# Five groups of the first attention pass get a second load of x in strips of 32 channels, turned on VectorE, and GpSimd folds softmax sums

## The chip, the cores and the metric

The kernel runs on one core of a Trainium2 chip as one program. Its time is the device time of one execution in microseconds (us). Engines: PE is TensorE (matmuls; PEld is its weight loads), DVE is VectorE, ACT is ScalarE, POOL is GpSimd, SP is SyncE, which issues nearly all DMAs. Each engine works through its own list of instructions in a fixed order.

## The reference, cut to what matters

The work is an induced-set attention over x (4 batches, 11456 tokens, 128 channels, float32) with 32 inducing rows, and behind it a mixture of experts (8 experts) for the tokens whose skip score is positive:

```python
def mab(q, kv):
    s = scale * (q @ kv.transpose(0, 2, 1))
    s = s - s.max(-1, keepdims=True)
    a = np.exp(s)
    a /= a.sum(-1, keepdims=True) + 1e-09
    return a @ kv
h = mab(I, x)                 # 32 rows per batch: first pass over x
x = mab(x, h)                 # every token against h: second pass over x
do_compute = x @ w_skip > 0
e_idx = argmax(x[do_compute] @ w_gate); gate_w = its softmax probability
out = x; out[do_compute] += gate_w * (relu(x @ w1[e]) @ w2[e])
```

The host lays x out transposed, xT[b, channel, token], and the output is written transposed too.

## The kernel before, in words

A batch has 11456 tokens, cut into 5 groups of 2048 and one of 1216 (NG = 6). The tile of a group holds 128 channels on the partitions and its tokens in the free dimension; four streams of 512 tokens (Q = 4) are worked on together, so that 4 times 32 inducing rows fill 128 partitions. The names of the steps:

- `load` (line 353): two DMAs of 512 KB per group into a tile `x`. There are XB = 12 such tiles, the groups of two batches. A tile is free again when the second pass has read it.
- `first`: scores `I x` (PE, line 372), running maxima per partition (DVE, 378), exponentials `a` (ACT, 382). For the sum `a x`, tokens must lie on the partitions. So `xt` turns x with 16 PE transposes of 128x128 (407) into PSUM banks, and four copies bring them into an SBUF tile `xt` (`xtc`: ACT line 335 or DVE line 337). `aT` turns `a` with four PE transposes (391), and one copy brings it into `a1T`. `hsum` (417) multiplies the two, and `add` (426) accumulates with a rescaling by `f`.
- `middle`, once a batch: brings the four streams' maxima together, makes `h` (`hr`, and `hc` turned), chooses the batch's expert (DVE, line 536, called the choose here), lets SP load that expert's weights `w1s`, `w2s` by the number just found, and makes the expert's rows `yr`.
- `second`, for each group: scores (PE, 693), a transpose in blocks of 32x32 (DVE, 698), row maxima (700), the subtraction (704, POOL or DVE), exponentials (ACT, 707), their sum and its reciprocal (DVE, 711, 713), the normalisation (716, POOL or DVE), a transpose back (721), then the gate of the expert (`..._q`) and the scaling by it (820).
- `emit`: eight matmuls a group (872) into four banks, four copies `o` to SBUF (335 or 337), two stores (882).

What sets the order: every step is an `Op` with a cost for each engine that may run it. `best_order` reads a rank and a bias for each step from the string PLACES (three characters a step), and `in_order` places the steps one by one, choosing the engine where two are offered and giving out banks and buffers. The result is one fixed list for each engine; nothing is chosen at run time. The list is written for the whole program at once, so the second pass of one batch runs beside the first pass of the next. SP's list holds loads, stores and the weights in one order, and SP waits at each for what it needs.

In the rows of an order below, `x4` means four such instructions, `x_1_818` is a tile of group 1 (the last number only tells tiles apart), and `a_2_1_...` belongs to batch 2, group 1.

Of the kernel before, what the change touches and what calls it, by code (L numbers as in the profile page):

```python
# [16 lines left out]
P = 128  # L17
# [122 lines left out]
def best_order(ops, bufs):  # L140
# [44 lines left out]
def kernel(  # L185
# [39 lines left out]
    def bank(i):  # L225
        return banks[i]
# [97 lines left out]
    def act(w):  # L324
        return {"ACT": 0.22 + 0.37 * w / 512}
# [15 lines left out]
    def load(k, after):  # L341
        b, g = divmod(k, NG)
        s = bt[b]
        G = s.groups[g]
        st = Steps(k)
        buf = s.xbuf[g] = Buf("x")
        cut = G.s1[1:] if k == 0 else [GC // 2]
        cut = [0] + [c for c in cut if c < G.cols] + [G.cols]

        def go(o):  # L350
            t = s.x[g] = xp.tile([P, GC], F32, tag="x", name=f"x_{b}_{g}")
            for c, d in zip(cut, cut[1:]):
                nc.sync.dma_start(out=t[:, c:d], in_=xT[b, :, G.col0 + c:G.col0 + d])

        s.xin[g] = last["x"] = st.add({"SP": 0.08 * len(cut)}, go, after, behind=[last["x"]], take=[buf], size=G.cols * 0.512)
        return st


    def first(s, g):
# [88 lines left out]
    def middle(s):  # L448
# [222 lines left out]
    def second(s, G, x, main):  # L671
# [474 lines left out]
```

## Time and profile before

| | before |
|---|---|
| median of 3 runs | 225.86 us (225.54 to 226.64) |
| the profiled execution | 226.54 us, of which its span is 224.7 us |
| PE busy | 201.1 us (89% of the span) |
| DVE busy | 170.5 us (76%) |
| ACT busy | 140.8 us (63%) |
| POOL busy | 111.0 us (49%) |
| moved by DMA | 51.64 MB, mean 230 GB/s |
| mean granted clock of TensorE | 0.981 |

The span is what the trace covers; 1.8 us of the profiled execution lie outside it. A busy share is an average over the span. The program has five parts here, cut at the four chooses (line 536, at 42.0, 84.2, 140.3 and 178.4 us): stage 0 up to the first choose, stages 1 to 3 between chooses, stage 4 from the last choose to the end. In stage 0 first passes run, in stages 1 to 3 the second pass of one batch beside the first of the next, in stage 4 second passes.

### The profile page before, as it was taken

The numbers are of one execution on the slowest core, as the hardware profiler recorded it, in microseconds if no ns is written. First come the engines' busy times: TensorE is split into PE (matmuls) and PEld (weight loads), VectorE is DVE, ScalarE is ACT, GpSimd is POOL, SyncE is SP. The second block draws the span as 40 slices with busy tenths as digits, with TensorE's granted clock in tenths as the row PEclk, the third lists the DMA queues.
The fourth block names the chain that finished last, engine by engine and source line by source line (L and its number), as shares of the span: only waits on it lengthen the run. The fifth ranks groups of instructions, "written<-read, shape, count | busy, mean of one in ns | idle before, by whom it ended". The sixth has DMA issues, their size and how long they took to land.

```text
span 224.7 us, 6693 instructions
## 1 busy us (share of the span) xinstructions
PE 201.1 (89%) x2541; PEld 116.2 (52%) x2542; DVE 170.5 (76%) x444; ACT 140.8 (63%) x333; POOL 111.0 (49%) x284
## 2 busy tenths in 40 slices
PE   4899999989999999999999999989999979688630
PEld 1556767657368764543675647327585333233210
DVE  4363653659898997799888787989898989997640
ACT  2356476655598886766996864768785756346730
POOL 7000000222538668457366541357677879989610
PEclk9999999999999999999999999999999999999975
DMA  6999970086796027979993492454221867445692
GB/s 160 378 419 405 412 313 13 6 266 203 248 392 239 3 115 249 297 308 355 370 414 150 190 314 98 141 234 190 93 101 42 330 205 285 190 175 198 252 365 71
DMA packets 16614, 51.64 MB, mean 230 GB/s; under 512 B 1984, under 2 KB 4928, under 8 KB 16576
## 3 DMA queue, kind: packets, MB, share of 16 engines
q1 hardware_dynamic: 16288, 51.12, 61.4%
q8 instruction: 22, 0.36, 0.7%
q14 instruction: 16, 0.13, 0.2%
q10 hardware_dynamic: 288, 0.02, 0.1%
HBM read 27.68 MB, written 23.46 MB: 228 GB/s over the span
## 4 chain that ended last, share of the span: by engine, by line
PE 54%; POOL 11%; DVE 11%; DMA 10%; ACT 5%; issue 4%; SPq 1%; DVEq 0%; ACTq 0%; POOLq 0%
PE bank L407 16%; PE bank L872 12%; PE bank L417 8%; PE bank L372 6%; DMA w1s<-in_w_dram 4%; PE bank L391 3%; DMA x<-in_xT_dram 3%; ACT o L335 3%; PE bank L693 3%; DMA out_dram<-o 3%; POOL e L716 2%; POOL v L820 2%; DVE ts L700 2%; DVE e L698 2%; PE bank L778 2%
## 5 line engine op out<-in xcount | busy, mean ns | idle before, releaser
L407 PE MATMUL bank<-ident,x 128*128 128x128 f32 (+1 forms) x368 | 50.8, 281 | 1.0 <-DMA x<-in_xT_dram 0.8
L335 ACT COPY o<-bank 128x512 f32<-128x512 f32 (+1 forms) x80 | 40.9, 570 | 16.4 <-PE bank L872 14.4
L335 ACT COPY xt<-bank 128x512 f32<-128x512 f32 (+1 forms) x78 | 42.9, 591 | 10.9 <-PE bank L407 10.6
L704 POOL TENSOR_TENSOR e<-e,ts 128x512 f32<-128x512 f32 (+1 forms) x22 | 22.5, 1023 | 49.6 <-DVE cmx L536 37.5
L407 PEld LDWEIGHTS bank<-ident,x 128*128 128x128 f32 (+1 forms) x368 | 40.4, 141 | 12.7 <-issue 3.0
L872 PE MATMUL bank<-u,hr 32*128 32x512 f32 (+1 forms) x192 | 26.0, 608 | 3.4 <-ACT o L335 2.5
L716 POOL TENSOR_TENSOR e<-texp,ts 128x512 f32<-128x512 f32 (+1 forms) x19 | 18.9, 999 | 17.0 <-DVE ts L713 13.0
L820 POOL TENSOR_TENSOR v<-e,gs 128x512 f32<-128x512 f32 (+1 forms) x20 | 20.8, 1040 | 8.9 <-DVE gs L337 4.9
L417 PE MATMUL bank<-xt,a1T 128*32 128x129 f32 (+1 forms) x736 | 25.1, 275 | 0.0
L382 ACT ACTIVATE a<-bank,bias 128x512 f32<-128x512 f32 (+1 forms) x24 | 16.0, 666 | 14.5 <-DVE a L378 14.5
L372 PE MATMUL bank<-x,iT_sb 128*32 128x512 f32 (+1 forms) x192 | 24.8, 583 | 0.0
L872 PE MATMUL bank<-u,yr 32*128 32x512 f32 (+1 forms) x192 | 23.9, 565 | 0.7 <-DVE u L721 0.6
L417 PEld LDWEIGHTS bank<-xt,a1T 128*32 128x32 f32 (+1 forms) x736 | 19.3, 109 | 8.1 <-issue 3.8
L693 PE MATMUL bank<-x,hc 128*32 128x512 f32 (+1 forms) x192 | 22.8, 573 | 0.1
L707 ACT ACTIVATE texp<-e 128x512 f32<-128x512 f32 (+1 forms) x24 | 14.6, 609 | 10.9 <-POOL e L704 8.0
L378 DVE TENSOR_SCALAR_CACHE_REDUCE a<-bank,bias 128x512 f32<-128x512 f32 (+1 forms) x20 | 13.9, 693 | 5.5 <-PE bank L372 5.2
L698 DVE STREAM_TRANSPOSE e<-bank 128x512 f32<-128x512 f32 (+1 forms) x24 | 15.9, 664 | 2.1 <-PE bank L693 2.0
L721 DVE STREAM_TRANSPOSE u<-v 128x512 f32<-128x512 f32 (+1 forms) x24 | 15.9, 664 | 1.7 <-POOL v L820 1.6
L721 DVE STREAM_TRANSPOSE u<-e 128x512 f32<-128x512 f32 (+1 forms) x24 | 15.6, 661 | 1.1 <-POOL e L716 0.9
L700 DVE TENSOR_REDUCE ts<-e 128x16 f32<-128x512 f32 (+1 forms) x24 | 15.7, 653 | 0.8
L711 DVE TENSOR_REDUCE sums<-texp 128x16 f32<-128x528 f32 (+1 forms) x24 | 15.6, 648 | 0.9 <-ACT texp L707 0.9
L872 PEld LDWEIGHTS bank<-u,yr 32*128 32x128 f32 x192 | 9.8, 185 | 10.8 <-issue 5.8
(153 smaller groups left out, 293.9 us busy)
## 6 DMA issues: line engine op xcount, KB each, us to landing
x<-in_xT_dram SPq DMA_DIRECT2D x43, 512.0 KB, 8.1
out_dram<-o SPq DMA_DIRECT2D x40, 512.0 KB, 3.9
out_dram<-o SPq DMA_DIRECT2D x8, 304.0 KB, 4.7
w1s<-in_w_dram SPq DMA_DIRECT2D x4, 512.0 KB, 4.2
w2s<-in_w_dram SPq DMA_DIRECT2D x4, 512.0 KB, 4.9
x<-in_xT_dram SPq DMA_DIRECT2D x4, 152.0 KB, 2.8
x<-in_xT_dram SPq DMA_DIRECT2D x3, 96.0 KB, 9.1
iT_sb<-in_iT_dram ACTq DMA_DIRECT2D x1, 16.0 KB, 2.2
```

Of the source, the lines that this page charges most:

```text
L335: nc.scalar.copy(out=out, in_=in_)
L372: nc.tensor.matmul(ps[q * M:(q + 1) * M, 0:W], lhsT=iT_sb, rhs=s.x[g][:, G.s1[q]:G.s1[q] + W], start=True, stop=True)
L407: nc.tensor.transpose(out=px[0:w, q * P:(q + 1) * P], in_=s.x[g][:, o:o + w], identity=ident)
L417: nc.tensor.matmul(ph[q * M:(q + 1) * M, 0:P + 1], lhsT=st["aT"][0:w, i, q * M:(q + 1) * M], rhs=xts[bx.idx][0:w, i, q, :], start=(i == 0) ...
L693: nc.tensor.matmul(ps[q * M:(q + 1) * M, 0:W], lhsT=s.hc[:, 0:M], rhs=x()[:, G.s2[q]:G.s2[q] + W], start=True, stop=True)
L698: nc.vector.transpose(out=t[:, 0:W], in_=st["ps"][:, 0:W])
L700: nc.vector.tensor_reduce(out=mx[:, 0:nb], in_=blocks(t), axis=AX.X, op=ALU.max)
L704: on(o).tensor_tensor(out=blocks(t), in0=blocks(t), in1=wide(st["mx"]), op=ALU.subtract)
L716: on(o).tensor_tensor(out=blocks(st["e"]), in0=ev(M), in1=wide(st["i"]), op=ALU.mult)
L721: nc.vector.transpose(out=st[f"u{k}"][:, 0:W], in_=st[src][:, 0:W])
L820: on(o).tensor_tensor(out=blocks(u), in0=blocks(st["e"]), in1=wide(st["gm"]), op=ALU.mult)
L872: nc.tensor.matmul(bank(bp[q].idx)[:, 0:G.w1], lhsT=m[r, :], rhs=st[k][r, c], start=(k == "u1"), stop=(k == "u2"))
```

## The change

Batch 1's group 2 and groups 1 and 3 of batches 2 and 3 (STRIPS) are loaded a second time, into a tile `xq`: four DMAs, each into 32 partitions, which hold channel r, r + 32, r + 64 and r + 96 of one stream side by side. With that layout, transposes in blocks of 32x32 on DVE write the very tile `xt` that the PE transposes and copies made (`x_turned`, two instructions of 1024 elements a partition). `a` is turned by DVE as well (`a_turned`). As a 32x32 transpose keeps the streams apart and puts tokens in another order, all four streams of such a group use one maximum: `turn_bias` (PE), `least` (DVE), `spread` (PE) and `common` (ACT or DVE) make it, ahead of the exponentials. The number of x tiles goes from 12 to 10. `fold` may add the right half of a row's exponentials to the left half on POOL, so that DVE's sum reads 17 numbers per row in place of 33. PLACES is a new string for the whole program.

```diff
-    XB = min(12, 2 * NG)
+    XB = min(10, 2 * NG)
+    STRIPS = ((), (2,), (1, 3), (1, 3))
+            G.strips = G.g in STRIPS[b]
 PLACES = (
-    "6f04O07A08w08i07W4EO0Au2CN0BE07Z09L0CF0Dj0GS0Fj04V0BK09N0881AW0BU0EL06z4Fr0FV37b0As0BP02a06H00304q02F06Q05F23V01Q18B0603"
+    "Ez0Ad0DG09c0B70EU4FS0Bx3BB0HB4BM0Aq2CR09B0B50As02R08l07F07U3B209e3BJ07714n07t03b0AM12k05T02502n02A02w01H03z00u00w11U01F1"
...
+        if G.strips:
+            def strips(o):
+                t = G.xq_t = wk.tile([P, Q, GC // Q], F32, tag="xq", bufs=BUFS["xq"], name=f"xq_{b}_{g}")
+                for q in range(Q):
+                    c = G.col0 + G.s1[q]
+                    nc.sync.dma_start(out=t[q * M:(q + 1) * M], in_=xT[b, :, c:c + G.w1].rearrange("(i r) n -> r i n", i=Q))
+            G.xq_in = last["xq"] = st.add({"SP": 0.08 * Q}, strips, behind=[s.xin[g], last["xq"]], take=[G.xq], size=G.cols * 0.95)
...
+        def a_turned(o):
+            nc.vector.transpose(out=t.rearrange("p t c -> p (t c)"), in_=st["a"][:, 0:W])
+        def x_turned(o, h):
+            n = GC // Q // M // 2
+            nc.vector.transpose(out=xts[bx.idx][:, 2 * h:2 * h + 2, :, 0:P].rearrange("p i q (c r) -> p (i q) c r", c=Q),
+                                in_=G.xq_t.rearrange("p c (j n) -> p j c n", n=M)[:, n * h:n * (h + 1)])
...
+        if G.strips:
+            o = L.add({"PE": 0.2}, turn_bias, o_m, take=[f1])
+            o = L.add({"DVE": 0.27}, least, o, free=[f1])
+            o = L.add({"PE": 0.3}, spread, o, take=[f2])
+            o_m = o_b = L.add({"ACT": 0.2, "DVE": 0.17}, common, o, free=[f2])
...
+        def fold(o):
+            st["whole"] = o.eng == "DVE"
+            if not st["whole"]:
+                v = ev(2 * HALF)
+                nc.gpsimd.tensor_tensor(out=blocks(st["e"])[:, :, 0:HALF], in0=v[:, :, 0:HALF], in1=v[:, :, HALF:], op=ALU.add)
```

The order around batch 2's group 1 on PE before: two of its four transposes of x (line 407, `x_1_818`; the others stand further up), the turning of its `a` (391), and its sum (417).

```order
L503 MATMUL bank_72<-ident,hr_1230 128x128
L407 MATMUL bank_75<-ident,x_1_818 128x128 x4
L811 MATMUL bank_73<-lt_3_1173,rep 32x16 x4
L407 MATMUL bank_77<-ident,x_1_818 128x128 x4
L811 MATMUL bank_74<-lt_2_1012,rep 32x16 x4
L906 MATMUL bank_72<-ident,lo_1244 1x128
L391 MATMUL bank_73<-ident,a_2_1_1129 128x128 x4
L522 MATMUL bank_75<-ws_sb,hc_1266 128x8
L523 MATMUL bank_75<-ws_sb,hc_1266 128x9
L913 MATMUL bank_72<-lom_1285,ones 128x1
L372 MATMUL bank_77<-x_2_882,iT_sb 32x512 x4
L417 MATMUL bank_72<-xt_165,a1T_1_1277 32x129 x16
```

The same group on PE now, from the batch's middle (540) on: 403 is `turn_bias`, 412 is `spread`, and no row of lines 447 or 431 (the transposes of x and a) belongs to group 1.

```order
L540 MATMUL bank_76<-acc_690,rep 128x129
L403 MATMUL bank_73<-ident,bias_1_1217 1x128
L431 MATMUL bank_72<-ident,a_2_0_1103 128x128 x4
L840 MATMUL bank_70<-u_0_5_1079,lrq_171 32x128 x4
L387 MATMUL bank_77<-x_2_913,iT_sb 32x512 x4
L557 MATMUL bank_71<-ident,hr_1257 128x128
L412 MATMUL bank_73<-ones,mn_2_1_1268 32x1 x4
L457 MATMUL bank_72<-xt_166,a1T_0_1241 32x129 x16
```

The sixteen transposes of x and four of a are gone from PE, and two short steps stand in their place, the second of them behind a DVE step. On DVE, ahead of batch 2's middle (`den_2108`), before:

```order
L337 COPY o_5_0_2066<-bank_77 128x304
L337 COPY o_5_1_2074<-bank_76 128x304
L426 SCALAR_TENSOR_TENSOR acc_1225<-acc_1225,f_2_5_1941,bank_72 128x129
L337 COPY o_5_1_2074<-bank_74 128x304
L936 TENSOR_REDUCE marks<-gxs 128x1
L337 COPY gs_2_163<-bank_75 128x16
L378 TENSOR_SCALAR a_3_3_2084,bias_3_2100<-bank_71,bias_2_2044 128x512
L490 TENSOR_SCALAR den_2108<-bank_75 128x1
```

On DVE, ahead of the same middle (`den_1974`) now; 424 is `x_turned`:

```order
L466 SCALAR_TENSOR_TENSOR acc_1326<-acc_1326,f_2_5_1832,bank_73 128x129
L783 STREAM_TRANSPOSE u_1_2_1947<-v_1_2_1927 128x512
L424 STREAM_TRANSPOSE xt_167<-xq_1_1631 128x8x128 x2
L544 TENSOR_SCALAR den_1974<-bank_75 128x1
L545 RECIPROCAL den_1974<-den_1974 128x1
L864 TENSOR_REDUCE gs_1_159<-qexp_124 128x16
```

Three copies `o` left DVE here, and both halves of batch 3's group 1 are turned directly in front of the middle. On SP, the loads of batch 3 and the weights of batch 2 before (`x_3_1834` is group 3; 882 are stores):

```order
L353 DMA x_3_1834<-in_xT_dram 128x1024 x2
L353 DMA x_4_1849<-in_xT_dram 128x1024 x2
L882 DMA out_dram<-o_3_0_1893 128x1024
L882 DMA out_dram<-o_3_1_1910 128x1024
L882 DMA out_dram<-o_1_0_1985 128x1024
L353 DMA x_5_2026<-in_xT_dram 128x1024
L353 DMA x_5_2026<-in_xT_dram 128x192
L882 DMA out_dram<-o_1_1_2009 128x1024
L882 DMA out_dram<-o_5_0_2066 128x2x304
L882 DMA out_dram<-o_5_1_2074 128x2x304
L547 TENSOR_LOAD ei_2172
```

On SP now (368 is the second load, 945 are stores):

```order
L358 DMA x_1_1609<-in_xT_dram 128x1024 x2
L368 DMA xq_1_1631<-in_xT_dram 32x4x512 x4
L358 DMA x_2_1696<-in_xT_dram 128x1024 x2
L945 DMA out_dram<-o_0_0_1723 128x1024
L945 DMA out_dram<-o_0_1_1728 128x1024
L358 DMA x_3_1773<-in_xT_dram 128x1024 x2
L368 DMA xq_3_1782<-in_xT_dram 32x4x512 x4
L945 DMA out_dram<-o_1_0_1839 128x1024
L945 DMA out_dram<-o_1_1_1868 128x1024
L945 DMA out_dram<-o_3_1_1977 128x1024
L945 DMA out_dram<-o_3_0_1967 128x1024
L358 DMA x_4_2024<-in_xT_dram 128x1024 x2
```

Batch 3's group 4 now stands last ahead of the expert number of batch 2, and its group 5 follows behind that batch's weights.

## Rows read from the trace of the kernel before

**Rows 1.** Page: busy us, share of the span, instructions per engine.

```profile
span 224.7 us, 6693 instructions
...
PE 201.1 (89%) x2541; PEld 116.2 (52%) x2542; DVE 170.5 (76%) x444; ACT 140.8 (63%) x333; POOL 111.0 (49%) x284
```

**Rows 2.** Page: chain that ended last, shares by engine.

```profile
PE 54%; POOL 11%; DVE 11%; DMA 10%; ACT 5%; issue 4%; SPq 1%; DVEq 0%; ACTq 0%; POOLq 0%
```

**Rows 3.** Windows by stage: length, busy us per engine, granted clock, DMA share, GB/s.

```profile
0.00:42.00 42.00, 37.91 (x428) 25.42 (x430) 19.49 (x44) 22.20 (x48) 4.04 (x39) 1.00 0.74 281
42.00:84.20 42.20, 41.03 (x591) 26.58 (x592) 36.25 (x98) 29.87 (x74) 21.00 (x47) 1.00 0.56 195
84.20:140.30 56.10, 55.62 (x740) 31.51 (x733) 47.81 (x131) 39.64 (x92) 30.18 (x71) 1.00 0.76 276
140.30:178.40 38.10, 36.91 (x486) 20.70 (x484) 34.24 (x89) 27.59 (x68) 24.95 (x56) 1.00 0.40 153
178.40:224.70 46.30, 29.59 (x317) 11.99 (x309) 32.72 (x86) 21.49 (x51) 30.86 (x74) 0.91 0.59 223
```

**Rows 4.** Lines by form: busy, mean ns of one, idle before; PE transposes and copies.

```profile
L407 PE MATMUL bank<-ident,x 128*128 128x128 f32 x352 | 48.9, 281 | 1.0 <-DMA x<-in_xT_dram 0.8
L335 ACT COPY xt<-bank 128x512 f32<-128x512 f32 x75 | 41.2, 591 | 9.9 <-PE bank L407 9.6
...
L391 PE MATMUL bank<-ident,a 128*128 128x128 f32 x88 | 14.2, 281 | 0.0
...
L337 DVE COPY xt<-bank 128x512 f32<-128x512 f32 x13 | 8.7, 679 | 3.1 <-PE bank L407 3.1
```

**Rows 5.** Lines by form: DVE transposes out of SBUF, a least, four small matmuls.

```profile
L721 DVE STREAM_TRANSPOSE u<-v 128x512 f32<-128x512 f32 x20 | 13.9, 696 | 1.5 <-POOL v L820 1.4
...
L721 DVE STREAM_TRANSPOSE u<-v 128x320 f32<-128x320 f32 x4 | 2.0, 509 | 0.2 <-POOL v L820 0.2
...
L467 DVE TENSOR_REDUCE mn<-bank 1x32 f32<-1x128 f32 x4 | 1.0, 262 | 0.0
...
L474 PE MATMUL bank<-ones,mn 1*32 1x1 f32 x32 | 1.0, 175 | 0.1
```

**Rows 6.** Lines by form: sums on DVE, normalisations on POOL and DVE.

```profile
L716 POOL TENSOR_TENSOR e<-texp,ts 128x512 f32<-128x512 f32 x16 | 16.8, 1050 | 14.3 <-DVE ts L713 10.3 <-ACT f L385 3.8
...
L711 DVE TENSOR_REDUCE sums<-texp 128x16 f32<-128x528 f32 x20 | 13.6, 682 | 0.4 <-ACT texp L707 0.4
...
L716 DVE TENSOR_TENSOR e<-texp,ts 128x512 f32<-128x512 f32 x4 | 2.8, 694 | 0.2
...
L716 POOL TENSOR_TENSOR e<-texp,ts 128x320 f32<-128x320 f32 x3 | 2.2, 722 | 2.6 <-DVE ts L713 2.6
...
L711 DVE TENSOR_REDUCE sums<-texp 128x10 f32<-128x330 f32 x4 | 1.9, 483 | 0.5 <-ACT texp L707 0.5
```

**Rows 7.** Lines by form: output copies and matmuls, first scores, scalings.

```profile
L872 PE MATMUL bank<-u,hr 32*128 32x512 f32 x160 | 22.8, 637 | 2.2 <-ACT o L335 1.3 <-DVE o L337 0.9
L872 PE MATMUL bank<-u,yr 32*128 32x512 f32 x160 | 21.0, 592 | 0.6 <-DVE u L721 0.6
L372 PE MATMUL bank<-x,iT_sb 128*32 128x512 f32 x160 | 20.5, 600 | 0.0
...
L820 POOL TENSOR_TENSOR v<-e,gs 128x512 f32<-128x512 f32 x17 | 18.6, 1095 | 8.6 <-DVE gs L337 4.9 <-ACT gs L335 3.3
...
L337 DVE COPY o<-bank 128x512 f32<-128x512 f32 x11 | 7.3, 673 | 1.5 <-PE bank L872 1.4
...
L337 DVE COPY o<-bank 128x304 f32<-128x304 f32 x5 | 2.3, 470 | 1.1 <-DMA out_dram<-o 1.1
```

**Rows 8.** Windows of two other stretches.

```profile
12.00:40.00 28.00, 27.84 (x359) 19.38 (x354) 14.42 (x35) 16.79 (x38) 0.00 (x0) 1.00 0.76 302
184.00:204.00 20.00, 16.03 (x191) 6.27 (x188) 18.12 (x43) 10.69 (x27) 18.17 (x40) 1.00 0.54 210
```

**Rows 9.** Page: DMA issues, count, KB each, median us from issue to landing.

```profile
w1s<-in_w_dram SPq DMA_DIRECT2D x4, 512.0 KB, 4.2
```

More of the change, by code (lines that the diff above doesn't have):

```diff
@@ L215, in split @@
             G.quarters = G.nb == MAXB and b < B - 1
+            G.strips = G.g in STRIPS[b]
+            assert not G.strips or G.cols == GC
         return groups
@@ L385, in exps, with turn_bias, least, spread @@
                 nc.scalar.activation(out=f, in_=st["old"], func=AF.Exp, scale=-1.0, bias=st["bias"])
+        def turn_bias(o):
+            nc.tensor.transpose(out=bank(f1.idx)[0:1, 0:P], in_=s.bias, identity=ident)
+        def least(o):
+            st["mn"] = wk.tile([1, M], F32, tag="mn1", bufs=8, name=f"mn1_{b}_{g}")
+            nc.vector.tensor_reduce(out=st["mn"], in_=bank(f1.idx)[0:1, 0:P].rearrange("o (q m) -> o m q", m=M), axis=AX.X,
+                                    op=ALU.min)
+        def spread(o):
+            for q in range(Q):
+                nc.tensor.matmul(bank(f2.idx)[q * M:(q + 1) * M, 0:1], lhsT=st["mn"], rhs=ones[0:1, 0:1], start=True, stop=True)
+        def common(o):
+            s.bias = st["bias"] = wk.tile([P, 1], F32, tag="bias1", bufs=8, name=f"bias1_{b}_{g}")
+            copy(o, s.bias, bank(f2.idx)[:, 0:1])
+        def a_turned(o):
+            t = st["aT"] = wk.tile([P, GC // Q // P, P], F32, tag="a1T", name=f"a1T_{b}_{g}")
+            nc.vector.transpose(out=t.rearrange("p t c -> p (t c)"), in_=st["a"][:, 0:W])
[3 more added lines that the diff above has]
+                                in_=G.xq_t.rearrange("p c (j n) -> p j c n", n=M)[:, n * h:n * (h + 1)])
         def aT(o):
@@ L430, in first @@
         o_m = L.add({"DVE": dve(W)["DVE"] + 0.1}, maxima, o_s, s.lastm)
-        o_e = L.add({"ACT": act(W)["ACT"] + (0.29 if g else 0.0)}, exps, o_m, s.laste, free=[bs])
-        cs = []
-        for i, (c, w) in enumerate(G.tb):
+        o_b = o_m
+        if G.strips:
+            f1, f2 = Buf("ps"), Buf("ps")
+            o = L.add({"PE": 0.2}, turn_bias, o_m, take=[f1])
+            o = L.add({"DVE": 0.27}, least, o, free=[f1])
+            o = L.add({"PE": 0.3}, spread, o, take=[f2])
+            o_m = o_b = L.add({"ACT": 0.2, "DVE": 0.17}, common, o, free=[f2])
+        o_e = L.add({"ACT": act(W)["ACT"] + (0.29 if g else 0.0)}, exps, o_b, s.laste, free=[bs])
+        cs = []
+        for h in range(2 if G.strips else 0):
+            last["xt"] = L.add({"DVE": 0.17 + 1.06}, lambda o, h=h: x_turned(o, h), G.xq_in, last["xt"],
+                               take=[bx] if h == 0 else [], free=[G.xq] if h == 1 else [])
+            cs.append(last["xt"])
+        for i, (c, w) in enumerate(G.tb if not G.strips else []):
             bp = Buf("ps")
@@ L438, in first @@
             cs.append(L.add({**act(512), **dve(512)}, lambda o, i=i, bp=bp: xtc(o, i, bp), o_x, free=[bp]))
-        o_a = L.add({"PE": 0.1 + 0.11 * len(G.tb)}, aT, o_e, take=[ba, et], free=[ea])
-        o_c = L.add({**act(P * len(G.tb)), **dve(P * len(G.tb))}, aTc, o_a, free=[ba])
+        if G.strips:
+            o_c = L.add(dve(W), a_turned, o_e, take=[et], free=[ea])
+        else:
+            o_a = L.add({"PE": 0.1 + 0.11 * len(G.tb)}, aT, o_e, take=[ba, et], free=[ea])
+            o_c = L.add({**act(P * len(G.tb)), **dve(P * len(G.tb))}, aTc, o_a, free=[ba])
         o_h = L.add({"PE": 0.24 * len(G.tb)}, hsum, o_c, *cs, take=[bh], free=[bx, et])
@@ L686, in second @@
         st["bufs"].append(bex)
+        half = {"POOL": 0.2 + 0.85 * nb * HALF / 512, "DVE": dve(W)["DVE"] - dve(nb * HALF)["DVE"]}
         def scores(o):
@@ L826, in second @@
         o = L.add(act(W), exps, o, take=[bex])
-        o = L.add({"DVE": dve(W)["DVE"] + 0.28}, total, o)
+        o = L.add(half, fold, o)
+        o = L.add({"DVE": dve(nb * HALF)["DVE"] + 0.28}, total, o)
         s.o_total.append(o)
```

70 lines of the change are left out of this document (37 added, 33 removed).

## The prediction, made before the changed kernel ran

> **What bounds the kernel now.** I read the page's head first [rows 1]: PE is busy 89% of the span and DVE 76%. The chain that ended last [rows 2] lies 54% on PE and 11% each on DVE and POOL. An average hides the stages, so I cut the span at the four chooses [rows 3]. In stages 1 to 3 PE is busy 41.0 of 42.2, 55.6 of 56.1 and 36.9 of 38.1 us: PE leads, and a stage lasts 0.5 to 1.2 us longer than its PE work. DVE is second there: 36.3, 47.8 and 34.2 us, or 86, 85 and 90%. In stage 4 no first pass is left; its middle shows two engines that share the lead, DVE 18.1 and POOL 18.2 of 20.0 us [rows 8]. So taking work off PE shortens stages 1 to 3 only until DVE stops it, and the question is what DVE gets in exchange.
>
> **The change, whole program.** Counts come from the two orders, durations from rows. PE loses 80 transposes of x, 48.9/352 = 0.139 us each of busy time (they overlap, so busy over count and not the mean), 11.1 us, and 20 of a at 14.2/88 = 0.161, 3.2 us [rows 4]. It gains 5 bias turns (as one transpose's mean, 0.281 us [rows 4]) and 20 spreads; a plain matmul of the order has two records in the trace, so 40 x 1.0/32 us [rows 5]: 2.7 us. Net -11.6 us.
>
> DVE gains ten `x_turned`. No row has 1024 elements; 512 take 696 ns and 320 take 509 [rows 5], so 0.974 ns an element over 197 ns: 1.19 us, 11.9 in all. Bounds: 1.0 us (no fixed part) and 1.39 (two of 512). The new output pattern is that of the `xt` copies, which take 679 ns where plain `o` copies take 673 [rows 4, 7], so the pitch of 129 costs nothing that shows. Five `a_turned` at 0.696 and five `least` at 0.262 [rows 5] make 4.8. DVE loses 4 copies `xt` (2.7), a net 8 long copies `o` (5.4) and 2 short ones (0.9) [rows 7], smaller copies (0.7), four normalisations or subtractions that go to POOL (two at 0.694, two short ones: 2.4) and what folding saves. The order fixes 16 folds, so "may" is settled. A sum over 33 numbers a row takes 682 ns for 16 rows and 483 for 10 [rows 6], 1.005 ns an element over 151; over 17 numbers that is 0.425 and 0.322, so 13 x 0.257 + 3 x 0.161 = 3.8 us saved. DVE: +16.7 - 15.9 = +0.8 us. It pays for the PE transposes with its copies.
>
> ACT loses 16 copies `xt` and 5 `a1T` at 0.59 and takes DVE's `o` copies at about the same price and five small ones [rows 4]: -5 us. It is off the path and stays there. POOL gains 13 folds at 0.64 and 3 at 0.47 (slope 1.71 ns an element over 175 ns, by its 1050 and 722 ns [rows 6]), 9.7 us, and 3.5 us of normalisations: 111 becomes 124 us. That is hidden where POOL has half its time free, in stages 1 and 2 [rows 3]; in front of the sum it lengthens each group's own chain by 0.64 - 0.26 = 0.4 us, which other groups cover while five `e` buffers are in flight. Without that cover it would cost up to 16 x 0.4 = 6 us.
>
> **By stage.** An order fixes which work lies between two chooses, so I count each stage by itself. Stage 0 [rows 3]: PE -12 transposes, -1.7; I take -1.2, since its start is filled by the first loads. Stage 1: PE -8 of x and -8 of a (-2.4), but the output matmuls of two groups come in, 16 with two records each at 22.8/160 or 21.0/160 us [rows 7], +4.4: with small ones 41.0 + 1.9 = 42.9. DVE gets four `x_turned`, two `a_turned`, two `least` (6.7) and loses two copies `o`, three folds' worth and three normalisations (4.2); moved work is +1.5: 36.3 + 4.0 = 40.3. Stage 2: PE -32 of x and -12 of a (-6.4), and three groups' scores (24 records at 20.5/160 [rows 7], -3.1), two groups' outputs (-4.4) and some short ones leave it (-2.0): 55.6 - 15.9 = 39.7. DVE +5.7 for the new steps, -4.8 for eight `o` copies, -2.1 for `xt` and `a1T`; three maxima and two scalings of some 0.7 each (as the two-input pass of [rows 6]) and small steps leave (-9.1): 47.8 - 10.3 = 37.5. Stage 3: PE -28 of x (-3.9), moved work +8.3: 41.3. DVE +4.3 new, -1.4 folds, +2.8 moved: 34.2 + 5.7 = 39.9. Stage 4: DVE takes three scalings (0.69 against POOL's 1.095 [rows 6, 7]) and loses some small steps, +1.6; POOL -4 after its folds.
>
> How long does a stage last over its busiest engine? With one leader 0.5 to 1.2 us [rows 3]; with two that are equal 20.0/18.2, 10% [rows 8]. Now all three stages have DVE within 2.6 us of PE, so each lies between: stage 1 44.1 to 47.2, stage 2 40.9 to 43.7, stage 3 42.5 to 45.4. I take 45.0 and 43.6 for stages 1 and 3. Stage 2 has a third bound. It moves 276 GB/s at a share of 0.76 [rows 3], so a full share moves 363; its new list on SP holds 13.7 MB of plain transfers and two second loads of 1.05 MB: 43.5 us, where before it was 42.6 of 56.1. I take 43.5. Sum 132.1 against 136.4: -4.3. Stage 4: POOL's relief and DVE's load, -1.5 to +1.6; I take +0.5.
>
> A second load in 32 partitions has no row. Lower bound: the rate of the plain loads, 302/0.76 = 397 GB/s [rows 8], 2.6 us each; upper: a weight load of 512 KB lands 4.2 us after its issue [rows 9], two of these with no overlap 8.4. I take 2.9, stage 2's own rate, which the 43.5 us hold already, and charge 1.0 us more for waits, between 0 and 6.
>
> [...]
>
> The added waits. `least` and `spread` stand in DVE's and PE's fixed lists: what is behind `spread` on PE (the next group's sum in the excerpt) waits if DVE is late. Four to eleven PE rows lie between, more than the 0.26 us of `least`, so I cost them at nothing; bare, some 1 us for each of five groups. `x_turned` waits for a DMA at the head of DVE's list; behind batch 3's group 1 stands batch 2's middle.
>
> Sum: -1.2 - 4.3 + 0.5 + 1.0 = -4.0 us on the profiled 226.54 us (span 224.7 and 1.8 around it): 222.5. The profiled execution stood 0.7 above the median of 225.86, so the median should be 221.8.
>
> **Rivals.** (a) DMA-bound second loads: slower. Place: stage 2. Halfway between my bounds of 2.6 and 8.4 a second load costs 5.5 us, 2.6 over what I took; stage 2's transfers are then 43.5 + 5.2 = 48.7 us, the strips reach DVE late in front of batch 2's middle, and the weights, with batch 3's group 5 behind them, queue up too. Each of five loads then holds up what is behind it by 2.6 us, 13 in all; half of that on the path gives 228.3, and with the last loads' latency 229. It decides once a second load takes over about 4 us or `x_turned` waits over 1 us for a DMA. For it: the full share of stage 2, and only ten x tiles. Against: shares of 0.56 and 0.40 in stages 1 and 3. (b) DVE takes the bound over as PE is relieved: the three stages at their upper ends, 47.2 + 43.7 + 45.4 = 136.3, give back what they gained; with the other terms +0.2 us, 226.0. For it: DVE and PE within 7% of each other in all three. Against: DVE reached 90% in stage 3 beside a PE at 97% [rows 3]. (c) More is gained: 44.1 + 42.0 + 42.5 in stages 1 to 3, -7.8, stage 0 -1.7, stage 4 -0.5, no wait: about 216. For it: each stage ran within 1.2 us of PE's work before.
>
> That the change doesn't do what it says is not open: the twenty second loads, ten turns and sixteen folds stand in the order.
>
> **How the numbers follow.** My forecast 0.49 (its own range 218.5 to 224.5), (c) 0.13, (b) 0.17, (a) 0.21. Half a percent, 1.1 us, is what a measurement can tell from no change, so faster 0.62, within it 0.17, slower 0.21. The range leaves about a tenth on either side: 216.5 to 228.5, where `x_turned` at 1.39 us (+2) and the fold without cover lie inside.
>
> **What would show it.** Right: PE about 189 us busy, DVE 171, POOL near 124; `x_turned` near 1.2 us; stage 2 near 44 us in place of 56; stages 1 and 3 longer than before. Wrong: second loads that land 5 us or more after issue with DVE idle in front of line 424 (a); `x_turned` well above 1.4 us, or DVE at 95% with PE idle in stages 1 and 3 (b); PE waiting at `spread` (line 412).

## The result, and the profile after the change

The changed kernel takes 223.39 us (median of 4 runs, 222.52 to 223.99) beside 225.7 us for the kernel before in the same session: ratio 0.9895 [0.986, 0.993], faster by 2.3 us. A second set of runs of the same kernel gave 222.38 beside 225.5, ratio 0.9855 [0.9811, 0.9898], faster by 3.1 us. The forecast was 4.0 us. Each ratio leaves out executions that were over 1.5% above the fastest of the same kernel. Direction and range held; the gain is some 0.6 to 0.8 of what the sum gave. The two profiled executions took 223.1 and 221.95 us, one on either side of the 222.5 forecast for a profiled one.

The head of the page, and the chain that ended last, of the changed kernel:

```profile
span 221.4 us, 6617 instructions
...
PE 195.9 (89%) x2486; PEld 106.5 (48%) x2487; DVE 173.1 (78%) x445; ACT 135.6 (61%) x328; POOL 124.5 (56%) x306
...
PE 48%; DVE 16%; POOL 15%; DMA 9%; issue 4%; ACT 3%; SPq 1%; POOLq 0%; DVEq 0%
```

Against [rows 1, 2] PE fell by 5.2 us (forecast 11.6), DVE rose by 2.6 (forecast 0.8), POOL by 13.5 (forecast 13), and the chain moved in part from PE to DVE and POOL.

The stages of the changed kernel, cut at its own four chooses, with the columns of [rows 3] (length, busy us and instructions of PE, PEld, DVE, ACT and POOL, granted clock, DMA share, GB/s):

```profile
0.00:39.20 39.20, 35.91 (x412) 23.65 (x414) 19.77 (x45) 20.17 (x43) 4.12 (x41) 1.00 0.85 285
39.20:84.55 45.35, 43.84 (x634) 25.70 (x635) 39.82 (x107) 30.57 (x78) 29.25 (x62) 1.00 0.85 260
84.55:128.82 44.27, 43.03 (x560) 22.68 (x559) 39.98 (x100) 33.12 (x82) 29.47 (x60) 1.00 0.98 331
128.82:174.89 46.07, 43.69 (x586) 23.26 (x582) 39.03 (x111) 30.23 (x77) 33.25 (x75) 0.96 0.51 198
174.89:221.40 46.51, 29.47 (x305) 11.23 (x305) 34.49 (x87) 21.45 (x49) 28.39 (x69) 0.91 0.58 218
```

Stage 2 shrank from 56.10 to 44.27 us, stages 1 and 3 grew from 42.20 to 45.35 and from 38.10 to 46.07, stage 0 lost 2.8. Read the last two columns too: stage 2 now runs at a DMA share of 0.98, where it had 0.76. In the profile of the second set stages 1 to 4 are:

```profile
40.04:85.97 45.93, 43.84 (x634) 25.65 (x635) 39.81 (x106) 30.57 (x78) 29.27 (x62) 1.00 0.84 258
85.97:129.52 43.55, 43.04 (x560) 22.68 (x560) 39.99 (x100) 33.11 (x82) 29.49 (x60) 1.00 0.99 333
129.52:173.19 43.67, 42.06 (x586) 22.64 (x582) 39.00 (x111) 30.15 (x77) 33.23 (x75) 1.00 0.54 210
173.19:220.20 47.01, 30.73 (x305) 11.78 (x305) 34.67 (x87) 21.46 (x49) 28.48 (x69) 0.88 0.57 216
```

The same program, but stage 3 is 2.4 us shorter, at a granted clock of 1.00 in place of 0.96; the low clock came in stage 4 instead, 0.88 beside 0.91, where PE is busy 1.26 us longer. Stage 3 in four of the experiments below: e1 and e2, which make all five second loads into 32 partitions, then e6 and e8, which leave three of them out or write them over 128 partitions:

```profile
129.08:175.97 46.89, 43.60 (x586) 23.15 (x582) 39.90 (x111) 30.34 (x77) 29.46 (x69) 0.96 0.52 196
129.52:175.79 46.27, 41.98 (x586) 22.65 (x582) 38.87 (x110) 30.11 (x77) 33.27 (x75) 1.00 0.55 199
```

```profile
130.48:173.57 43.09, 41.92 (x586) 22.73 (x582) 38.92 (x110) 30.20 (x77) 33.12 (x75) 1.00 0.56 199
128.59:171.68 43.09, 41.89 (x586) 22.62 (x582) 38.89 (x111) 30.20 (x77) 33.11 (x75) 1.00 0.54 199
```

So the 46.07 us of the first profile are not a rare episode: stage 3 is a place where the slow second loads are paid for, in very different amounts: 3.0 us over e6 and e8 in the first profile and 0.6 in the second. Its windows further below show how.

The lines of the changed kernel that answer to [rows 4 to 6] (busy, mean ns of one, idle before and what ended it):

```profile
L447 PE MATMUL bank<-ident,x 128*128 128x128 f32 x272 | 37.9, 283 | 0.0
...
L424 DVE STREAM_TRANSPOSE xt<-xq 128x1024 f32<-128x1024 f32 x10 | 12.0, 1218 | 0.0
L431 PE MATMUL bank<-ident,a 128*128 128x128 f32 x68 | 11.3, 283 | 0.1
L768 POOL TENSOR_TENSOR e<-texp 128x272 f32<-128x272 f32 x13 | 9.0, 692 | 6.6 <-ACT texp L762 6.6
...
L772 DVE TENSOR_REDUCE sums<-e 128x16 f32<-128x272 f32 x13 | 5.5, 423 | 1.9 <-POOL e L768 1.7
...
L420 DVE STREAM_TRANSPOSE a1T<-a 128x512 f32<-128x512 f32 x5 | 3.3, 670 | 0.0
...
L412 PE MATMUL bank<-ones,mn 1*32 1x1 f32 x40 | 1.2, 174 | 0.5 <-DVE gs L822 0.5
```

`x_turned` takes 1.218 us (forecast 1.19) and DVE never stood in front of it: idle 0.0, so the second load was always there in time. PE waits 0.5 us once in front of `spread`. The folded sum takes 423 ns, 2 ns from the forecast; the fold itself 692 ns, 50 over it.

What a second load takes shows where the first one runs. Windows of the changed kernel, same columns, at 24 us with plain loads and from 26 us with the loads `xq` of 32 partitions:

```profile
24.00:26.00 2.00, 2.00 (x44) 1.75 (x47) 0.00 (x0) 1.63 (x4) 0.00 (x0) 1.00 1.02 407
26.00:27.00 1.00, 1.00 (x12) 0.26 (x8) 0.37 (x2) 0.00 (x0) 0.00 (x0) 1.00 1.06 188
27.00:28.00 1.00, 1.00 (x11) 0.38 (x4) 0.88 (x3) 0.22 (x1) 0.00 (x0) 1.00 1.08 201
28.00:29.00 1.00, 1.00 (x12) 0.96 (x10) 0.62 (x2) 1.00 (x3) 0.00 (x0) 1.00 1.05 203
29.00:30.00 1.00, 1.00 (x10) 0.76 (x8) 0.81 (x2) 1.00 (x3) 0.00 (x0) 1.00 1.11 215
30.00:31.00 1.00, 1.00 (x15) 0.65 (x13) 0.22 (x2) 1.00 (x4) 0.00 (x0) 1.00 1.03 217
```

The share stays full and the rate halves, 407 to about 205 GB/s: by that rate 1.05 MB take some 5.1 us, where I had 2.9. In the second profile the same five windows show 182 to 252 GB/s, 219 on average, or 4.8 us.

Windows of the same kernel round the start of batch 2's middle in stage 3:

```profile
135.00:136.00 1.00, 0.73 (x8) 0.00 (x0) 0.93 (x4) 1.00 (x3) 0.48 (x2) 1.00 0.80 246
136.00:137.00 1.00, 0.59 (x16) 0.34 (x16) 0.97 (x4) 0.82 (x2) 0.40 (x2) 1.00 0.96 356
137.00:138.00 1.00, 0.05 (x4) 0.08 (x8) 0.93 (x4) 0.00 (x0) 0.73 (x2) 1.00 1.03 422
138.00:139.00 1.00, 1.00 (x12) 0.65 (x16) 0.68 (x2) 0.00 (x0) 1.00 (x2) 0.53 1.02 410
139.00:141.00 2.00, 2.00 (x10) 0.38 (x3) 0.19 (x1) 1.90 (x7) 0.84 (x4) 0.50 1.02 413
141.00:142.00 1.00, 1.00 (x10) 0.83 (x12) 0.97 (x2) 0.48 (x2) 0.00 (x0) 0.77 1.07 432
```

And from its chain (start, length, what) and PE's timeline there:

```profile
131.21 6.61 DMA w1s<-in_w_dram
...
137.95 1.04 PE L644 MATMUL bank<-w1s,hc 128*32 128x256 f32 x8 [1.18 <-DMA w1s<-in_w_dram]
```

Batch 2's weights were 6.61 us on the way; the median before was 4.2 [rows 9], and the longest of the four 4.5. PE ran dry at 135 to 138 us, and the granted clock then stood at 0.50 to 0.53 for three microseconds and at 0.77 for a fourth while PE was fully busy. PE's busy time in stage 3 is 43.69 here and 42.06 in the second profile: 1.6 of the 2.4 us are the clock, the other 0.8 idle time. In e1 the same weights took 7.44 us, PE waited 1.6 us for them, and the clock fell there too (0.96 over the stage). In e6 and e8 no `w1s` took over 4.9 us, and PE did not wait for it in stage 3. A wait for weights is not new: PE's waits for `w1s` in the kernel before, then in the changed one (us, times, longest):

```profile
PE bank L590 <- DMA w1s<-in_w_dram: 1.8, 3, 1.1
```

```profile
PE bank L644 <- DMA w1s<-in_w_dram: 2.3, 2, 1.2
```

In the sum over the program these waits grew by only 0.5 us (by 0.3 in the second profile); what makes stage 3 long is the lull in one place, with the low clock behind it where that came.

### The profile page after: what moved, and what is told of

Its sections match the earlier page's. It is cut to its first block, busy times and chain, and to the rows that moved or that the text cites. A ratio compares the mean times of both kernels' runs of the same rounds, so it can differ in the third digit from the quotient of the medians.

```text
span 221.4 us, 6617 instructions
## 1 busy us (share of the span) xinstructions
PE 195.9 (89%) x2486; PEld 106.5 (48%) x2487; DVE 173.1 (78%) x445; ACT 135.6 (61%) x328; POOL 124.5 (56%) x306
## 4 chain that ended last, share of the span: by engine, by line
PE 48%; DVE 16%; POOL 15%; DMA 9%; issue 4%; ACT 3%; SPq 1%; POOLq 0%; DVEq 0%
PE bank L447 11%; PE bank L935 9%; PE bank L387 7%; PE bank L457 7%; DMA w1s<-in_w_dram 5%; PE bank L748 5%; DMA out_dram<-o 4%; DVE u L783 4%; PE bank L431 3%; POOL e L778 3%; DVE ts L755 2%; DVE e L753 2%; POOL v L882 2%; POOL e L768 2%; POOL e L759 1%
## 5 line engine op out<-in xcount | busy, mean ns | idle before, releaser
L340 ACT COPY o<-bank 128x512 f32<-128x512 f32 (+1 forms) x90 | 45.5, 570 | 14.7 <-PE bank L935 9.2
L340 ACT COPY xt<-bank 128x512 f32<-128x512 f32 (+1 forms) x62 | 33.9, 590 | 10.0 <-PE bank L447 9.6
L447 PE MATMUL bank<-ident,x 128*128 128x128 f32 (+1 forms) x288 | 39.7, 282 | 0.0
L447 PEld LDWEIGHTS bank<-ident,x 128*128 128x128 f32 (+1 forms) x288 | 31.9, 142 | 9.2 <-issue 2.0
L387 PE MATMUL bank<-x,iT_sb 128*32 128x512 f32 (+1 forms) x192 | 25.8, 582 | 1.1 <-ACT o L340 1.1
L778 POOL TENSOR_TENSOR e<-texp,ts 128x512 f32<-128x512 f32 (+1 forms) x22 | 22.1, 1004 | 7.4 <-DVE ts L775 4.8
L748 PE MATMUL bank<-x,hc 128*32 128x512 f32 (+1 forms) x192 | 24.9, 593 | 0.1
L882 POOL TENSOR_TENSOR v<-e,gs 128x512 f32<-128x512 f32 (+1 forms) x20 | 19.9, 1001 | 6.4 <-ACT gs L340 4.6
L783 DVE STREAM_TRANSPOSE u<-v 128x512 f32<-128x512 f32 (+1 forms) x24 | 16.1, 671 | 2.2 <-POOL v L882 1.9
L935 PEld LDWEIGHTS bank<-u,yr 32*128 32x128 f32 x192 | 9.3, 184 | 11.9 <-issue 5.8
L768 POOL TENSOR_TENSOR e<-texp 128x272 f32<-128x272 f32 (+1 forms) x16 | 10.5, 656 | 7.7 <-ACT texp L762 7.7
```

What stands on the lines that cost most here:

```text
L340: nc.scalar.copy(out=out, in_=in_)
L387: nc.tensor.matmul(ps[q * M:(q + 1) * M, 0:W], lhsT=iT_sb, rhs=s.x[g][:, G.s1[q]:G.s1[q] + W], start=True, stop=True)
L447: nc.tensor.transpose(out=px[0:w, q * P:(q + 1) * P], in_=s.x[g][:, o:o + w], identity=ident)
L748: nc.tensor.matmul(ps[q * M:(q + 1) * M, 0:W], lhsT=s.hc[:, 0:M], rhs=x()[:, G.s2[q]:G.s2[q] + W], start=True, stop=True)
L778: on(o).tensor_tensor(out=blocks(st["e"]), in0=ev(M), in1=wide(st["i"]), op=ALU.mult)
L783: nc.vector.transpose(out=st[f"u{k}"][:, 0:W], in_=st[src][:, 0:W])
```

## The experiments

Theory A: the second loads, at half the rate, are what is missing from the gain. Theory B: DVE, near its limit, takes it. Theory C: the new wait on POOL's folds takes it. Ratios are to the kernel before, which ran on the same chip each time (225.5 to 225.8 us).

**Fewer second loads (e6_loads_once).**

```diff
...
+                if len(once) == BUFS["xq"]:
+                    G.xq_t = once[g // 2]
+                    return
...
```

> Three of the five second loads are left out (batch 2's group 3 and batch 3's groups 1 and 3 turn the data of an earlier group, so their part of the sum is another one); every instruction of PE, DVE, ACT and POOL stays. Theory A: about 15 us of DMA time go, stage 2 falls from 44.3 us by 2 to 4, the weights of batch 2 land in 4.4 us, and the time falls by 3 to 5 us, to about 219. Theory B (DVE bounds it): the time stays within 1 us of 223.4.

Measured 221.27 us, 0.98 [0.9755, 0.9846]: by the ratios 2.1 us below the first set of the changed kernel and 1.2 below the second, whose interval it overlaps. Twelve of the twenty DMAs of the second loads are worth no more than that, and theory A's 3 to 5 us did not come. Stage 2 is at a DMA share of 0.79 there and takes 44.98 us, no less than in the changed kernel; what got shorter is stage 3 (43.09 us).

**Second loads over all partitions (e8_all_partitions).** As many bytes and DMAs, in rows of 2 KB as before, but each DMA writes 128 partitions.

```diff
-  nc.sync.dma_start(out=t[q * M:(q + 1) * M], in_=xT[b, :, c:c + G.w1].rearrange("(i r) n -> r i n", i=Q))
+  nc.sync.dma_start(out=t[:, q, :], in_=xT[b, :, c:c + G.w1])
```

> The second loads keep their 1.05 MB, their four DMAs and their rows of 2 KB, but each DMA writes all 128 partitions (the channels as they lie in memory), so the five groups' part of the sum is a wrong one. If the 32 partitions are the cause of the rate near 205 GB/s, the rate goes to about 400, stage 2's DMA share falls from 0.98 to about 0.87, and the time falls by 1 to 2.1 us, up to what leaving three second loads out gave. If rows of 2 KB are the cause, rate and time stay.

Measured 220.22 us, 0.9751 [0.9708, 0.9794], beside 0.9855 [0.9811, 0.9898] for the changed kernel in the same set: 2.2 us. Its first second load, same columns:

```profile
26.00:27.00 1.00, 1.00 (x20) 0.40 (x16) 0.35 (x1) 0.00 (x0) 0.00 (x0) 1.00 1.05 408
27.00:28.00 1.00, 1.00 (x13) 0.16 (x6) 0.76 (x2) 0.00 (x0) 0.00 (x0) 1.00 1.13 432
28.00:29.00 1.00, 1.00 (x10) 1.00 (x11) 0.76 (x2) 0.97 (x3) 0.00 (x0) 1.00 0.98 393
```

The full rate is back, so the number of partitions that a load writes made the half rate, not its bytes or the length of its rows. (The order in which the rows are read changed with it; no run changes that alone.) PE has no wait for `w1s` in this trace. Its stage 2:

```profile
84.51:128.59 44.08, 43.03 (x560) 22.67 (x559) 39.99 (x101) 33.08 (x82) 29.40 (x60) 1.00 0.92 343
```

Freed to a share of 0.92, stage 2 is no shorter than 43.55 or 44.27: it lies on PE's 43.03. Stages 0, 1 and 3, with 39.46, 45.05 and 43.09 us, are 0.6 to 0.9 us shorter than in the second profile of the changed kernel; against the first profile it is stage 3 that differs, by 3.0 us.

**Weights ahead of a load (e2_weights_first).** Batch 3's load of group 4 is issued behind batch 2's weights.

```diff
...
+        late, w = bt[3].xin[4], bt[2].o_w
+        steps.remove(late)
+        steps.insert(steps.index(w) + 1, late)
...
```

> Only batch 3's group 4 is issued behind batch 2's weights on SP, not ahead of them. Theory A (stage 3 lost its time to late weights): in the changed kernel w1s of batch 2 landed 6.6 us after its issue, PE waited 1.2 us for it and then ran 3.5 us at a granted clock of 0.5. Without the 1 MB ahead it lands about 2.5 us earlier, the wait and the low clock go, and the time falls by 1.5 to 3 us, to about 221. Theory B (stage 3 is bound by DVE, which was 85% busy there): DVE fills what PE gives back, and the time moves by less than 0.7 us. If group 4 itself comes late, slower than the changed kernel by up to 2 us.

Measured 223.56 us, 0.9892 [0.9854, 0.9931]: nothing gained. The clock in stage 3 is 1.00 and PE's busy time 41.98 us, yet the stage lasts 46.27. Its chain, and two of its waits there (who waits for whom: us, times, longest):

```profile
134.88 9.43 DMA out_dram<-o
```

```profile
ACT o L340 <- DMA out_dram<-o: 3.6, 1, 3.6
...
PE bank L447 <- ACT o L340: 3.1, 1, 3.1
```

The queue was as full as before: the share is 0.91 to 1.04 from 136 to 146 us. The longest weight load fell from 6.6 to 5.0 us, and a store came late instead, so an `o` buffer stayed taken and PE waited behind ACT. One victim was changed for another. PE's clock beside that wait, same columns as the windows above:

```profile
142.00:143.00 1.00, 0.00 (x0) 0.00 (x0) 1.00 (x4) 0.00 (x0) 0.75 (x4) 1.00 1.08 434
143.00:144.00 1.00, 0.00 (x0) 0.00 (x0) 0.49 (x2) 0.00 (x0) 0.00 (x0) 1.00 0.99 397
144.00:145.00 1.00, 0.15 (x1) 0.16 (x2) 0.00 (x0) 0.62 (x3) 0.00 (x0) 1.00 1.03 408
145.00:146.00 1.00, 1.00 (x24) 0.83 (x27) 0.00 (x0) 1.00 (x5) 0.28 (x1) 1.00 1.00 407
```

PE does nothing for nearly three microseconds and finds its clock at 1.00 when it goes on; in the changed kernel's first profile a shorter lull was followed by 0.50. So here stage 3 is 46.27 us long by idle time alone.

**Two queues (e5_two_queues).** Strips 2 and 3 of each second load are issued by ACT, and the strips in the order 0, 2, 1, 3.

```diff
-                for q in range(Q):
+                for q in (0, 2, 1, 3):
...
-                    nc.sync.dma_start(out=t[q * M:(q + 1) * M], in_=...)
+                    (nc.sync if q < 2 else nc.scalar).dma_start(out=t[q * M:(q + 1) * M], in_=...)
```

> Streams 0 and 1 of each second load are issued by SP, streams 2 and 3 by ACT, on two queues that run side by side. Theory A: partitions 0 to 63 and 64 to 127 are then written at once, the rate of a second load goes from 205 towards 400 GB/s, stage 2 (DMA share 0.98) gets shorter, and the time falls by 1 to 2.5 us, less ten DMA issues of about 0.35 us that ACT now carries. If the rate limit is in the reading of rows of 2 KB and not in the partitions written, the rate stays near 205 and the time within 0.5 us or worse for ACT's issues. Theory B: no change.

Measured 229.26 us, 1.0173 [1.0124, 1.0222], slower than before. A wait of ACT that the changed kernel's trace does not have:

```profile
ACT xt L340 <- DMA x<-in_xT_dram: 6.8, 1, 6.8
```

ACT's list is fixed; a DMA in it that had to wait for an earlier load held up the copies behind it, for 6.8 us. Stage 2 took 52.75 us. The edit doesn't tell what two queues would give, only what it costs to put them on a busy engine.

**Strips in the order 0, 2, 1, 3 (e3_interleave)**, issued by SP alone.

```diff
-                for q in range(Q):
+                for q in (0, 2, 1, 3):
```

> The four DMAs of each second load are issued in the order of streams 0, 2, 1, 3, so that two that follow each other write partitions 64 apart. In the changed kernel the first second load ran at about 205 GB/s with the DMA engines full. If the limit is which partitions are written at a time, and two queued DMAs overlap, the rate rises to 250 to 400 GB/s and the time falls by 0.5 to 1.5 us. If each engine takes its queue strictly in turn, rate and time stay (within 0.5 us of 223.4). Theory B: time stays whatever the rate.

Measured 222.69 us, 0.9853 [0.9805, 0.9901]: not to be told from the changed kernel. From 26 to 31 us its rate was 193, 238, 221, 256 and 258 GB/s, 233 on average, where the changed kernel's two profiles have 205 and 219: a small gain of rate at most, and nothing that the time shows.

**Each turn made twice (e4_turn_twice).**

```diff
+            for _ in range(2):
             nc.vector.transpose(...
```

> Each turn of a second load is done twice: ten more passes of 1.2 us on DVE, 12.2 us, nothing else. If DVE were the bound of stages 1 to 3, all of it shows: 8 to 12 us, 231 to 235. If DVE's 85 to 90% leave room beside PE and the DMAs, a part shows: 3 to 7 us.

Ratio 1.0191 [1.0122, 1.026], which is 230.0 us: 12.2 us more of DVE work cost 6.6 us beside the first set, about half, and 5 to 8 us by the interval. Its stages 1 and 2:

```profile
39.08:86.56 47.48, 44.11 (x634) 25.80 (x635) 44.06 (x109) 31.21 (x80) 29.30 (x62) 1.00 0.83 249
86.56:134.28 47.72, 43.37 (x560) 22.56 (x556) 44.51 (x106) 32.77 (x81) 29.50 (x60) 1.00 0.97 307
```

At 44.06 and 44.51 us DVE stands level with PE's 44.11 and over its 43.37, and both stages last 7 to 8% longer than DVE's work. In the changed kernel DVE has 4.2 and 4.5 us less there, so it is second, but not by much: theory B is how the next microsecond of DVE work would be paid, not what took the gain.

**No fold (e1_no_fold).**

```diff
-            st["whole"] = o.eng == "DVE"
+            st["whole"] = True
```

> The changed kernel without the folds: DVE sums all 33 numbers of a row, the rest and the order stay. DVE gets 3.8 us more, POOL loses 10.5 us. If DVE has become the bound (theory B), the time rises by 2 to 4 us, to 226 or 227. If DMA sets stages 2 and 3 (theory A), DVE's extra is hidden and the time stays within 1 us of 223.4. A third view: in the second half of stage 3 POOL runs without a gap from 156 to 165 us, and a fold lies on that chain; then the time falls by 1 to 2 us.

Measured 223.36 us, 0.9862 [0.9826, 0.9897]: no difference. DVE was busy 176.7 us in place of 173.1 and POOL 114.7 in place of 124.5. So in the new order the folds are worth nothing on balance; a gain on DVE and a loss on POOL that cancel are not ruled out.

**The fold alone (e7_fold_alone)**: the same 16 folds put into the kernel before, in its own order.

```diff
...
+                nc.gpsimd.tensor_tensor(out=half, in0=v[:, :, 0:HALF], in1=v[:, :, HALF:], op=ALU.add)
+                nc.vector.tensor_reduce(out=r[:, 0:nb], in_=half, axis=AX.X, op=ALU.add)
...
```

> The kernel before with the same 16 sums folded on POOL, right ahead of the sum, in the order of before: DVE loses 3.8 us, POOL gets 10. If the fold brought the gain, 223 to 224. I expect no gain: PE leads stages 1 to 3 there, and each fold lengthens its group's chain by 0.4 us, so 225.5 to 227.5.

Measured 234.28 us, 1.0401 [1.0356, 1.0446]: a miss, 8.6 us slower although DVE's busy time fell from 170.5 [rows 1] to 168.6 us. DVE's largest wait (line 716 is the fold here, 717 the sum):

```profile
DVE sums L717 <- POOL e L716: 13.5, 12, 2.2
```

In the old order the sum stands close behind the exponential; with a fold between, DVE stands 12 times for POOL, up to 2.2 us. In the changed kernel, where the order places fold and sum by themselves, the same wait is 1.7 us (line 772 above). Theory C holds for the fold without its order and not for the change.

**Both small edits (e9_interleave_no_fold)**, strips in the order 0, 2, 1, 3 and no folds.

```diff
+                for q in (0, 2, 1, 3):
...
+            st["whole"] = True
```

> Second loads issued in the order of streams 0, 2, 1, 3, and no folds. Each alone came out within noise of the changed kernel (222.7 and 223.4). If the interleaved rate is real it stays near 222.5; if the two were noise, near 223.4.

Measured 222.93 us, 0.9822 [0.9761, 0.9882]: within the interval of the changed kernel. No version that computes the same output beat the changed one by more than the intervals.

**The changed kernel once more (e10_after_again)**, without an edit, in one set with e8 and e9; its time and stages stand in the section on the result.

> The changed kernel itself on the same chip as the two others, to compare with: 222.5 to 224.

## Why the prediction was right, and which terms were mis-sized

*The stages.* Without the 1.0 us of waits, forecast 40.8, 45.0, 43.5, 43.6 and 46.8 us; the first profile has 39.2, 45.35, 44.27, 46.07 and 46.51, the second 40.04, 45.93, 43.55, 43.67 and 47.01. The mechanism, PE's transposes out of the full stage 2 and moved work into stages 1 and 3, is right in its main line: stages 1 to 3 shrank with PE's work in them, from 136.4 us to 133.2 and 135.7. Stages 1 to 3 with the 1.0 us of waits were to last 133.1 us; they lasted 135.7 and 133.2.

*PE, -11.6 us: the step furthest off.* The rows that the change touches did what I counted: the transposes of x are 37.9 and 2.4 us (with 16 of 48 columns) where they were 48.9 [rows 4] and 2.5, those of a 11.3 where they were 14.2, and the bias turns and spreads add 2.6, so these rows fell by 11.4. But the busy times of all PE MATMUL groups add up to 222.2 where they added up to 229.7, 7.5 us less: the other groups hold 3.9 us more, the scores of the second pass above all (20.3 to 21.9), which ran in part at the low clock. And the page's head, in which overlapping work counts once, fell by only 5.2. The second profile has 222.0 and 195.5 us, with its low clock in stage 4. Stage 2 shows the error without the clock, at 1.00 in both kernels: its groups add up to 65.7 us before and 49.6 after, 16.1 less where I had counted 15.9, but PE was busy 55.62 and 43.03, 12.6 less. The other 3.5 us of what was taken out had lain over a neighbour's work. Dividing a group's busy time by its count removes the overlap inside the group and not that with other groups. So stage 2 held 43.0 us of PE, not 39.7. Its length came out right for another reason than mine: I put 43.5 us of transfers there, and e8 and e6, with the share at 0.92 and 0.79 and the stage no shorter, show that PE's 43.03 is what it lies on. That a bound which did not hold came out near the one that did is luck, and by it the error of this term did not reach the sum.

*The second load, 2.9 us with 1.0 us for waits: the term by which the sum was off.* It took about 5.1 us, worked out from 205 GB/s, where I had taken stage 2's own rate with no row of a load into 32 partitions. What the partitions are worth is shown by e8: 393 to 432 GB/s over 128 of them beside 188 to 217 over 32 in the changed kernel. The price on the time was about 2 us (2.2 by e8, 1.2 to 2.1 by e6) where I charged 1.0, and much of it falls in stage 3: 46.07 and 43.67 us with the loads into 32 partitions, 43.09 in e8 and in e6, where I had 43.6 without waits. The difference is about 1 of the 0.9 to 1.7 us by which the two measured gains fall short of the forecast; the rest is within their intervals.

*Rival (a)*, 229 us, had its mechanism right and its price wrong. Its condition, a second load of over about 4 us, was met, and late weights came, yet the kernel was not slower. DVE's idle time ahead of line 424 is 0.0: the strips were issued early enough, and the backlog reached only what stood behind them, the weights or, in e2, a store.

*Rival (b)*, DVE as the bound, did not come: DVE is at 87 to 92% in stages 1 and 2 and 85 to 89% in stage 3 over the two profiles, and PE above it each time. By e4 about half of each microsecond added to DVE would show; in e1 3.6 us more on DVE, with POOL 9.8 us lighter, did not. *Rival (c)*, 216 us, did not come either: its stages were PE's work with hardly a wait, and PE's work was longer.

*DVE, +0.8 us*, came out at +2.6, mostly in stage 2: 39.98 against 37.5; stages 1 and 3 hold 39.8 and 39.0 against 40.3 and 39.9. *The folds*, 3.8 us off DVE, were counted rightly in busy time and are worth nothing in time (e1); their cover, for which I set up to 6 us, is the new order: without it they cost 8.6 (e7). *The added waits* of `least` and `spread`, costed at nothing, measured 0.5 us on PE, in one place.

*Open:* what brings the low clock. It fell in stage 3 in the first profile and in e1, in stage 4 in the second profile, and not after the longer lull of e2. And no run separates the turning on DVE from the rest of the change: the order is new throughout and the x tiles are ten in place of twelve, so how much of the 2.3 to 3.1 us either of these gives or takes is not shown.

## What to carry to other kernels

Before a group's busy time is taken off an engine, compare the sum of all groups with the engine's own busy time: where the sum is larger, only part of each group's time is there to be freed. When a transfer's shape is not in the trace, ask how many partitions it reaches and not only how many bytes (here 188 to 217 GB/s into 32 and, in e8, 393 to 432 into 128); and look at who is queued behind it, since the load's own reader may lose nothing; here the weights, or a store, came late behind it. An extra step in front of an instruction of a fixed list can be free in one order and dear in another (the folds: no measured difference without them in e1, 8.6 us in the old order in e7), so test the two together.

## What the runs showed of the hardware

- Loads into 32 partitions moved 188 to 217 GB/s with the DMA share full (182 to 252 in the second profile); the same bytes in rows of the same length into 128 partitions moved 393 to 432.
- After PE had been busy 0.73, 0.59 and 0.05 of three microseconds, its granted clock stood at 0.50 to 0.53 for about 3 us and was back at 1.00 from 142 us on, with PE fully busy all the while. PE was busy 43.69 us in that stage beside 42.06 in the second profile, where the clock there was 1.00: 1.6 us. After 0.78, 0.00, 0.00 and 0.15 in e2 it stayed at 1.00. In stage 4 of the second profile it stood at 0.50 to 0.59 after 0.80, 0.49 and 0.00 (a mean of 0.82 from 185 to 190 us and of 0.84 from 190 to 195); in the first profile, after 0.64, 0.49 and 0.00 there, it stayed at 1.00.
- In e5 a DMA issued in ACT's list, waiting for an earlier load, held ACT's copies up for 6.8 us.
